# Turning tokens 1 and 3 of the last group in shifted blocks, with the other copy of the output weights, and a new issue order for the tail

## Chip, cores, metric

The kernel runs on one core of a Trainium2 chip. The metric is the device time of one launch in microseconds (us), the median of several runs; lower is better. About 0.2% (0.3 us) is what a measurement of this kernel can tell from no change.

## What is computed

Two independent layers over 2048 tokens of width 448 (bf16), their outputs side by side in one `[1, 2048, 896]` tensor. Part A is a diagonal state-space layer (448 complex states, a scan over the sequence, projections in and out, a skip term). Part B is local attention with 16 heads of width 28, where each token looks at 8 keys spaced 2 apart:

```
# part A
h   = Lam_bar * h + B_bar @ x[t]                 # for t in 0..2047, complex
y   = 2 * real(C @ h) + x * Dskip
# part B
q, k, v = split_heads(x @ wqkv)                  # 16 heads, 28 wide
idx     = pos[:, None] - 2 * arange(8)           # masked where negative
p       = softmax(q . k[idx] / sqrt(28))         # over the 8 keys
o       = sum_w p[w] * v[idx[w]]
b       = merge_heads(o) @ wo
out     = concat([y, b], -1)
```

## The kernel before, in words

**Tiling.** Partition p of an on-chip tile holds the tokens 16p to 16p+15, so the kernel speaks of 16 "tokens" j = 0..15, each a row of 448 numbers on 128 partitions. Part B works on four groups of four tokens: g = 3 (tokens 12 to 15), 2, 1 and 0, in that order.

**Part B's last stages** (`PartB.pv`, L787). For each group VectorE (DVE in the profile) forms attention times values and adds the products up: `mul` (L819) and `add` (L822) work on 3584 columns, two halves ("y") of 4 tokens x 448, and at the end the halves would be added (L838). For groups 3, 2 and 1 a DMA then transposes the sum (`trd`, L872, issued by SyncE, SP in the profile), and TensorE (PE) multiplies the result by the output weights (`rr` L900 and `mm` L908). For group 0, the last, there is no time for a DMA: its last addition is cut in two (L841, part 0 for tokens 0 and 1, part 1 for tokens 2 and 3), and TensorE turns each token itself (`tr`, L884): four blocks of 128 columns, each by two matmuls against the identity, which also add the two halves. ScalarE (ACT) copies the turned token from PSUM (`ev`, L889), TensorE multiplies it by the output weights (`mm`, L915, four matmuls), ScalarE copies the product out (`ev2`, L218 in the helper; for token 2 VectorE takes the last 192 columns, L222), and SyncE sends it away (`out`, L925).

448 columns are three blocks and a half. Before, token j's four blocks start at column 448j, so the fourth reaches 64 columns into the next token, and `wo_p[:, 3]` has zeros in its lower 64 rows, where those columns fall. `wo_p` holds a second copy of the weights in rows 4 to 7, displaced by 64, which groups 1 to 3 already use for odd tokens.

**Part A's end** (`PartA.outputs`, L1443). For each token, or pair of tokens, TensorE sums up `y_ps` (L1458, L1462), ScalarE copies it out (L218), or for tokens 12 to 15 VectorE adds the skip term while it copies (L1474, after L1439 has made the term from `Dskip`, loaded at L1429); SyncE sends it (L1477).

**PSUM.** One buffer of two banks (tag "W") and six of one bank (tag "s"). Every `y_ps`, `pt_o` (a turned token) and `wo_ps` (a product with the output weights) takes one of the six or the "W"; a matmul into a reused bank waits until the engine that emptied it is done.

**Order.** Each piece of work is a numbered unit, and `ORDER` (L51) lists all 685 by hand. The program is built in that order, so each engine executes its units in the order in which they stand there, and waits by semaphores for the others. Each engine is a queue: a unit that waits holds up all behind it.

Of the kernel before, what the change touches and what calls it, by code (L numbers as in the profile page):

```python
# [10 lines left out]
ALU = mybir.AluOpType  # L11
# [28 lines left out]
NC = 3  # L40
# [6 lines left out]
ADD = (0, 0, 0, 0, 0, 0, 0)  # L47
EADD = (0, 0, 0, 0)
# [51 lines left out]
def vec2(n):  # L100
    return n / 1920.0 + 0.07
# [219 lines left out]
class PartB:  # L321
# [464 lines left out]
    def pv(self, b, prio, deps):  # L786
# [13 lines left out]
        lasts, halves, trs = {}, {}, {}  # L800
        for r in (1, 0):
            last = getattr(self, "pv_last", None)
            half = getattr(self, "u_half", None)
            ahead = half is not None
            us = (5, 4, 1, 0)
            for n in range(4):

                def step(n=n, r=r, part=0, half=half):
                    alloc()
                    acc = self.acc[2 * b + r]  # L810
                    tmp = [acc] + [cx.pr[:, 4096 * i:4096 * i + 2 * n1] for i in range(3)]

                    def mul(i):
                        u = us[i]
                        o = j0 + 4 * r + DIL * u
                        w0 = 4 * (u // 4) + 2 * (u % 2)
                        aa = self.attn[b][:, w0:w0 + 2, :, r, :].rearrange("q y i h -> q (y i) h").unsqueeze(2).to_broadcast(
                            [NCH, 8, DH, H])
                        V.tensor_tensor(tmp[i].rearrange("p (j d h) -> p j d h", j=8, d=DH), aa, self.vd[:, o:o + 8], op=ALU.mult)  # L819

                    def add(i):
                        V.tensor_tensor(acc, acc, tmp[i], op=ALU.add)  # L822
                    if n == 0:
                        mul(1 if half else 0)
                        mul(2 if half else 1)
                    elif n == 1 and half:
                        mul(3)
                        mul(0)
                    elif n == 2 and half:
                        add(1)  # L830
                        add(2)
                    elif n < 3:
                        mul(n + 1)
                        add(n)
                    elif 2 * b + r > 0:
                        add(3)
                        if not EADD[2 * b + r]:
                            V.tensor_tensor(acc[:, n1:2 * n1], acc[:, 0:n1], acc[:, n1:2 * n1], op=ALU.add)  # L838
                    else:
                        a, t = (v.rearrange("p (y j c) -> p y j c", y=2, j=4)[:, :, 2 * part:2 * part + 2] for v in (acc, tmp[3]))  # L840
                        V.tensor_tensor(a, a, t, op=ALU.add)  # L841
                dd = []
                for u in us[:2 + ahead] if n == 0 else us[n + 1 + ahead:n + 2 + ahead] if n < 3 else ():
                    o = j0 + 4 * r + DIL * u
                    for p in range(o, o + 8):
                        dd += self.u_vh[p] if p < HALO else [self.u_v[p - HALO]]
                cost = 2 * vec2(2 * n1) if n < 3 else vec2(2 * n1) + vec2(n1) * (not EADD[2 * b + r]) if 2 * b + r > 0 else vec2(n1)
                last = P.add("DVE", cost, step, dd + [self.u_attn[b], last, *self.u_prod[0], *self.u_prod[1], *self.u_lg[0], *self.u_lg[1],
                                         *self.u_vm, *self.u_proj, *deps, half if n == 1 else None], prio - 0.1 * r)
            lasts[r] = [last, last]  # L850
            if 2 * b + r == 0:
                last = P.add("DVE", cost, lambda: step(part=1), [last], prio - 0.1 * r)
                lasts[r][1] = last
            self.pv_last = last
            g = 2 * b + r
            halves[g] = self.u_half = None
            if EADD[g]:

                def merge(g=g):
                    acc = self.acc[g]  # L860
                    nc.gpsimd.dma_start(acc[:, n1:2 * n1], acc[:, 0:n1], accum_op=ALU.add)
                halves[g] = self.u_half = P.add("POOL", 1.1, merge, [last], PRI["wo"], lat=3.5)
            if not hasattr(self, "u_first"):
                self.u_first = last
        for r in (1, 0):
            g = 2 * b + r
            if g > 0:

                def trd(g=g):
                    o = (0, 5376, 7168, 8960)[g]  # L870
                    t = self.oTd[g] = self.rb2[:, o:o + n1].rearrange("p (k q) -> p k q", q=NCH)
                    nc.sync.dma_start(t, self.acc[g][:, n1:2 * n1], transpose=True)  # L872
                trs[r] = P.add("SP", 1.7, trd, [halves[g] or lasts[r][1]], PRI["wo"], lat=3.6)
        for j in range(j0, j0 + JB):
# [3 lines left out]
            def tr(j=j, jb=jb):  # L878
                pt = jb["pt"] = self.psum.tile([NCH, KT, NCH], f32, name="pt_o", tag="s")
                a = j % 4 * D  # L880
# [22 lines left out]
            def mm(j=j, jb=jb, g=g, e=e):  # L903
# [10 lines left out]
                for kt in range(KT):  # L914
                    nc.tensor.matmul(ps[:], lhsT=o[:, kt, :], rhs=self.wo_p[:, kt, :],  # L915
                                     start=(kt == 0), stop=(kt == KT - 1))
# [27 lines left out]
class PartA:  # L944
# [261 lines left out]
    def scan(self, prio, qk_done):  # L1206
# [9 lines left out]
        for m in range(NM):  # L1216
# [99 lines left out]
            def carry(out, lt, Sc, hv, new=False):  # L1316
                mt(out[:, 0:NCH], lhsT=lt, rhs=Sc, start=new, stop=True, **kw)
                mt(out[:, NCH:512], lhsT=lt, rhs=hv[:, 3, 0:384], start=False, stop=True, **kw)
# [12 lines left out]
            def again(n, box=box, pair=pair):  # L1331
# [5 lines left out]

            def back(n, box=box, again=again, hget=hget):
                again(n)
                mt(box[2 * n], lhsT=cx.ident[:], rhs=hget()[:, 2 * n, :], start=True, stop=False, **kw)  # L1340

            def s6(box=box, Sc=Sc, L=L, hget=hget, again=again, add=bool(ADD[m])):
                if add:
                    again(0)
                carry(box[0], L(1), Sc, hget(), add)

            def s7(box=box, L=L, hget=hget, again=again, add=bool(ADD[m])):
                if add:
                    again(1)
                mt(box[2], lhsT=L(1), rhs=hget()[:, 1, :], start=add, stop=True, **kw)  # L1350

            def ctile(box=box):
                if "c" not in box:
                    box["c"] = pool.tile([NCH, 2, 512], bf16, name="cP", tag="cP", bufs=NC)
                return box["c"]

            def addin(box=box, hget=hget):
                nc.gpsimd.dma_start(hget()[:, 0::2, :], box["c"][:], accum_op=ALU.add)

            def evPf(box=box, hget=hget, ctile=ctile, add=bool(ADD[m])):  # L1360
                nc.scalar.copy(ctile()[:] if add else hget()[:, 0::2, :], box["P"][:])

            def evpf(n, box=box, hget=hget, ctile=ctile, add=bool(ADD[m])):
                nc.scalar.copy(ctile()[:, n, :] if add else hget()[:, 2 * n, :], box[2 * n])  # L1364
# [39 lines left out]
            add = bool(ADD[m])  # L1404
            if not hold[0] and not add:
                b0 = P.add("PE", pe(1, 512), lambda f=back: f(0), [b0], PRI["bk"] + m * 0.1, acq="W" if pair else "s")
            if not hold[pair ^ 1] and not add:
                b2 = P.add("PE", pe(1, 512), lambda f=back: f(1), [b2, b0], PRI["bk"] + m * 0.1, acq=None if pair else "s")
            v0 = P.add("PE", pe(2, 256), s6, [b0, u3], pc, acq=("W" if pair else "s", "cP") if add else None)
            v2 = P.add("PE", pe(1, 512), s7, [b2, u1, v0 if add and pair else None], pc, acq="s" if add and not pair else None)  # L1410
# [5 lines left out]
            if add:  # L1416
                w0 = w2 = P.add("POOL", 1.2, addin, [w0, w2], pc, rel="cP", lat=3.0)
# [91 lines left out]
def kernel(  # L1509
# [24 lines left out]
    plan = Planner({**BUFS, "fl": NF, "cP": NC, "PR": 3, "mx": 1, "ex": 1, "at": 1, "pw": 4, "oT": 3, "yb": 4, "ya": 8})  # L1534
# [64 lines left out]
```

## Time and profile before

| | |
|---|---|
| median of 3 runs | 139.94 us (139.92 to 139.99) |
| the profiled execution | 140.0 us, span of its instructions 138.3 us |
| busy: PE, DVE, ACT, POOL | 131.3, 123.0, 88.3, 17.7 us |
| mean granted TensorE clock | 0.997 |
| chain that ended last | DVE 39%, PE 38%, SP's queue 9%, issue 5% |
| last group's last addition (L841) ends | 128.57 us |
| last copy out of PSUM ends | 135.47 us |

The span goes from the first to the last instruction, so 1.7 us of the profiled execution lie around it. Positions below are microseconds from the span's start. In the chain of waits, "issue" is time in which the profile shows no cause; DVEq, SPq and so on are an engine's sequencer.

### The profile page before, as it was taken

To read this page: it belongs to the slowest core of one execution; us is meant where nothing else is said; L and a number is where in the kernel's file an instruction comes from. 1 tells how busy PE (TensorE), PEld (TensorE's weight loads), DVE (VectorE), ACT (ScalarE), POOL (GpSimd) and SP (SyncE) were. 2 spreads that over 40 slices of the span, in tenths; PEclk is the share of its full clock that TensorE was granted. 3 is DMA by queue.
4 is the path that set the end of the run, shared out by engine and by line. 5 is a ranking of instruction groups with operands and counts; after the bars stand their busy time and mean duration, and the time that the engine had idled before them with its cause. 6 is when DMAs were issued, how large, how long until landed. Compare 5 with 4: busy or idle time off the path is not lost.

```text
span 138.3 us, 2835 instructions
## 1 busy us (share of the span) xinstructions
PE 131.3 (95%) x1065; PEld 67.2 (49%) x1071; DVE 123.0 (89%) x134; ACT 88.3 (64%) x199; POOL 17.7 (13%) x69
## 2 busy tenths in 40 slices
PE   7999989999999999999999999999999999999790
PEld 2534334444455453656534563556565455445450
DVE  1369998899999999997999999999999999999920
ACT  3555587998554976657695998689547151721571
POOL 7589830025000000000000000000000000000000
PEclk9999999999999999999999999999999999999998
DMA  4968965658658525648899039350093425575163
GB/s 128 269 126 208 179 87 61 153 130 95 81 113 53 97 52 112 179 104 131 167 222 198 0 67 240 95 111 0 0 95 103 139 78 118 141 163 169 35 197 100
DMA packets 41694, 16.58 MB, mean 120 GB/s; under 512 B 33685, under 2 KB 41044, under 8 KB 41681
## 3 DMA queue, kind: packets, MB, share of 16 engines
q1 hardware_dynamic: 41618, 16.40, 57.6%
q8 instruction: 8, 0.13, 0.4%
q14 instruction: 5, 0.04, 0.1%
q10 hardware_dynamic: 63, 0.01, 0.0%
HBM read 4.32 MB, written 3.67 MB: 58 GB/s over the span
## 4 chain that ended last, share of the span: by engine, by line
DVE 39%; PE 38%; SPq 9%; issue 5%; ACT 3%; DMA 3%; DVEq 0%; ACTq 0%
DVE rb L822 11%; DVE prods L819 11%; SPq L366 6%; PE v_ps L760 6%; PE scb L1247 5%; DVE rb L819 4%; PE scp L1247 4%; PE logits L672 3%; DMA rb<-in_B_x_dram 3%; DVE pw L1197 2%; PE qk_ps L481 2%; DVE prods L656 2%; PE wo_ps L915 2%; DVE rb L838 2%; ACT qk L218 1%
## 5 line engine op out<-in xcount | busy, mean ns | idle before, releaser
L819 DVE TENSOR_TENSOR prods<-attn,vd 128x3584 bf16<-128x3584 bf16 x12 | 24.0, 2018 | 0.0
L822 DVE TENSOR_TENSOR rb<-rb,prods 128x3584 bf16<-128x3584 bf16 x11 | 22.2, 2019 | 0.1
L656 DVE TENSOR_TENSOR prods<-qk 128x3072 bf16<-128x3072 bf16 (+1 forms) x15 | 19.1, 1325 | 0.0
L481 PE MATMUL qk_ps<-rb 128*128 128x512 bf16 x60 | 14.4, 379 | 0.7 <-DMA rb<-in_B_x_dram 0.6
L1462 PE MATMUL y_ps<-Ccat,qk 128*128 128x448 bf16 x60 | 14.6, 352 | 0.0
L218 ACT CAST vd<-v_ps 128x448 bf16<-128x448 f32 x16 | 7.9, 540 | 5.2 <-PE v_ps L760 4.9
L1247 PEld LDWEIGHTS <-Bcat 128*128 128x128 bf16 x84 | 7.5, 100 | 7.4 <-issue 1.1
L1294 ACT CAST ubuf<-scb 128x64 bf16<-128x64 f32 x35 | 7.3, 220 | 5.9 <-PE scb L1301 3.5
L218 ACT CAST qk<-wo_ps 128x448 bf16<-128x448 f32 (+1 forms) x16 | 8.1, 529 | 4.5 <-PE wo_ps L908 2.8
L1462 PE MATMUL y_ps<-Ccat,h 128*128 128x448 bf16 x45 | 11.0, 353 | 0.0
L1247 PE MATMUL scb<-xaT_sb,Bcat 128*128 128x512 bf16 x42 | 10.9, 380 | 0.0
L218 ACT CAST qk<-y_ps 128x448 bf16<-128x448 f32 (+1 forms) x9 | 5.6, 663 | 8.2 <-issue 4.2
L760 PE MATMUL v_ps<-rb 128*128 128x448 bf16 x48 | 10.1, 353 | 0.0
L220 ACT ACTIVATE qk<-qk_ps 64x512 bf16<-64x512 f32 (+1 forms) x15 | 8.9, 599 | 1.7 <-PE qk_ps L488 1.3
L481 PEld LDWEIGHTS <-rb 128*128 128x128 bf16 x60 | 5.6, 98 | 7.8 <-issue 1.0
L660 DVE TENSOR_TENSOR prods<-qk 128x768 bf16<-128x768 bf16 (+3 forms) x18 | 9.1, 566 | 0.1
L1462 PEld LDWEIGHTS <-qk 128*128 128x128 bf16 x60 | 5.8, 98 | 5.3 <-ACT qk L1364 0.2
L819 DVE TENSOR_TENSOR rb<-attn,vd 128x3584 bf16<-128x3584 bf16 x4 | 8.1, 2021 | 0.1
L908 PE MATMUL wo_ps<-wo_p,rb 128*128 128x448 bf16 x36 | 8.1, 353 | 0.0
L1197 DVE TENSOR_TENSOR pw<-Dm,spair 128x1920 bf16<-128x1920 bf16 x7 | 8.1, 1150 | 0.0
L218 ACT CAST qk<-qk_ps 128x512 bf16<-128x512 f32 (+2 forms) x11 | 6.3, 585 | 2.5 <-PE qk_ps L488 1.1
L1247 PE MATMUL scp<-xaT_sb,Bcat 128*128 128x512 bf16 x30 | 7.8, 381 | 0.0
(197 smaller groups left out, 259.0 us busy)
## 6 DMA issues: line engine op xcount, KB each, us to landing
out_dram<-qk SPq DMA_DIRECT2D x32, 112.0 KB, 1.8
vd<-vd SPq DMA_DIRECT2D x3, 392.0 KB, 4.5
rb<-in_B_wqkv_dram SPq DMA_DIRECT2D x3, 336.0 KB, 4.5
qk<-in_A_x_dram SPq DMA_DIRECT2D x1, 448.0 KB
ra<-in_A_B_re_dram SPq DMA_DIRECT2D x1, 392.0 KB, 4.3
ra<-in_A_B_im_dram SPq DMA_DIRECT2D x1, 392.0 KB
rb<-in_A_C_re_dram SPq DMA_DIRECT2D x4, 98.0 KB, 2.9
rb<-in_A_C_im_dram SPq DMA_DIRECT2D x4, 98.0 KB, 3.5
```

What stands on the lines that cost most here:

```text
L218: nc.scalar.copy(out, in_)
L220: nc.scalar.mul(out, in_, scale)
L366: nc.sync.dma_start(self.xT[:, j], bass.AP(x.tensor, x.offset + j * D - DT, [[T * D, NCH], [1, KT * NCH]]), transpose=True)
L481: nc.tensor.matmul(out(n), lhsT=w(n, full, k), rhs=self.xT[:, j:j + 4, k, :], start=(not rfirst and k == 1), stop=(rfirst and k == KT - 1) ...
L656: V.tensor_tensor(out.rearrange("p i j k q -> p i (j k) q"), qq.unsqueeze(1).to_broadcast([NCH, 2, 4 * nk, NCH]), bass.AP(kk.tensor, kk.of ...
L660: V.tensor_tensor(jk(out[:, i, a:e]), qq, kk, op=ALU.mult)
L760: nc.tensor.matmul(box["ps"][:].rearrange("p h d -> p (h d)"), lhsT=self.xT[:, j, k, :], rhs=self.wv[:, k, :], start=False, stop=(k == KT ...
L819: V.tensor_tensor(tmp[i].rearrange("p (j d h) -> p j d h", j=8, d=DH), aa, self.vd[:, o:o + 8], op=ALU.mult)
L822: V.tensor_tensor(acc, acc, tmp[i], op=ALU.add)
L1197: V.tensor_tensor(t[:], self.o["Dm"][:].rearrange("p (a b) -> p a b", b=2).unsqueeze(1).to_broadcast([NCH, 2 * NPW, 32, 2]), self.sp[:, m ...
L1247: mt(box[i], lhsT=self.Bcat[:, k, m, :], rhs=self.xk(slice(i, None, 4), k), start=(i % 2 == 0 and k == 0), stop=False, **kw)
L1462: nc.tensor.matmul(ps, lhsT=h, rhs=self.Ccat[:, m, :], start=(m == 0 and not skip), stop=(m == NM - 1), skip_group_check=True)
```

## The change

Three things.

1. For tokens 1 and 3 of group 0 the four blocks start 64 columns earlier, at 448j - 64. The first block now begins in the token before, and the fourth ends with the token. The product uses rows 4 to 7 of `wo_p`. Token 1 then reads nothing of tokens 2 and 3. The number of instructions is the same.
2. The last nine lines of `ORDER` are rearranged. Group 0's tokens are turned in the order 0, 2, 1, 3 (1, 2, 3, 0 before), and outputs of part A, products of groups 1 to 3 and transfers change places.
3. Two options that the tables switch off for all steps (`ADD`, `EADD`, and the buffer `cP`) are taken out. They issued nothing.

```diff
-ADD = (0, 0, 0, 0, 0, 0, 0)
-EADD = (0, 0, 0, 0)
...
 ORDER = [
...
-    443, 405, 462, 463, 407, 440, 441, 409, 464, 465, 445, 402, 442, 466, 467, 444, 530, 403, 446, 404, 468,
+    443, 405, 462, 463, 407, 440, 441, 409, 464, 465, 445, 402, 442, 466, 467, 444, 530, 570, 531, 616, 403,
...
             def tr(j=j, jb=jb):
                 pt = jb["pt"] = self.psum.tile([NCH, KT, NCH], f32, name="pt_o", tag="s")
-                a = j % 4 * D
+                a = j % 4 * D - 64 * (j % 2)
...
                 for kt in range(KT):
-                    nc.tensor.matmul(ps[:], lhsT=o[:, kt, :], rhs=self.wo_p[:, kt, :],
+                    nc.tensor.matmul(ps[:], lhsT=o[:, kt, :], rhs=self.wo_p[:, 4 * (j % 2) + kt, :],
                                      start=(kt == 0), stop=(kt == KT - 1))
...
-                        if not EADD[2 * b + r]:
-                            V.tensor_tensor(acc[:, n1:2 * n1], acc[:, 0:n1], acc[:, n1:2 * n1], op=ALU.add)
+                        V.tensor_tensor(acc[:, n1:2 * n1], acc[:, 0:n1], acc[:, n1:2 * n1], op=ALU.add)
```

What the order of issue becomes, at three places. Line numbers of the changed kernel are 20 lower in the second half of `pv` (L884 becomes L864, L908 L888, L915 L895), 38 lower in `outputs`, 3 lower in the helper (L218 becomes L215).

First place, TensorE's last stretch, before. The numbers tell tiles apart: `pt_o_1792`, `1809`, `1825`, `1841` are tokens 1, 2, 3, 0 turned; `wo_ps_1744` is token 7's product, `wo_ps_1819`, `1853`, `1861`, `1868` are the products of tokens 1, 2, 3, 0. In brackets stand the engines whose semaphores the instruction waits for.

```order
L884 MATMUL pt_o_1792<-ident_63,rb_70 128x128 [waits Activation_49]
...
L884 LDWEIGHTS rb_70 [waits DVE_49]
...
L908 MATMUL wo_ps_1744<-wo_p_587,rb_70 128x448
...
L884 MATMUL pt_o_1809<-ident_63,rb_70 128x128 [waits Activation_49]
...
L915 MATMUL wo_ps_1819<-wo_p_587,rb_70 128x448 [waits DVE_49]
...
L884 MATMUL pt_o_1825<-ident_63,rb_70 128x128 [waits PE_49]
...
L884 MATMUL pt_o_1841<-ident_63,rb_70 128x128 [waits DVE_49]
...
L915 MATMUL wo_ps_1853<-wo_p_587,rb_70 128x448
...
L915 MATMUL wo_ps_1861<-wo_p_587,rb_70 128x448
...
L915 MATMUL wo_ps_1868<-wo_p_587,rb_70 128x448 [waits PE_49]
```

The same stretch now: `pt_o_1788`, `1806`, `1820`, `1830` are tokens 0, 2, 1, 3 turned; `wo_ps_1740` is token 7's product, `wo_ps_1815`, `1842`, `1852`, `1868` the products of tokens 0, 2, 1, 3.

```order
L864 MATMUL pt_o_1788<-ident_63,rb_70 128x128 [waits Activation_49]
...
L888 MATMUL wo_ps_1740<-wo_p_587,rb_70 128x448
...
L864 LDWEIGHTS rb_70 [waits DVE_49]
L864 MATMUL pt_o_1806<-ident_63,rb_70 128x128 [waits Activation_49]
...
L895 LDWEIGHTS rb_70 [waits Activation_49]
...
L864 MATMUL pt_o_1820<-ident_63,rb_70 128x128 [waits DVE_49]
...
L864 MATMUL pt_o_1830<-ident_63,rb_70 128x128 [waits PE_49]
...
L895 MATMUL wo_ps_1842<-wo_p_587,rb_70 128x448
...
L895 LDWEIGHTS rb_70 [waits DVE_49,Activation_49]
L895 MATMUL wo_ps_1852<-wo_p_587,rb_70 128x448
...
L895 MATMUL wo_ps_1868<-wo_p_587,rb_70 128x448 [waits PE_49]
```

Before, the first wait for VectorE that is not for the sum itself stands after two turned tokens, and one more turned token stands behind a second such wait. Now two turned tokens and a whole product stand ahead of the first, and the second stands ahead of the product of token 1.

Second place, ScalarE's last copies, before: `wo_ps_1626` is the product of token 11 (group 2).

```order
L218 CAST qk_109<-wo_ps_1740 128x448
L889 CAST rb_70<-pt_o_1792 128x512
L218 CAST qk_109<-wo_ps_1626 128x448
L218 CAST qk_109<-wo_ps_1744 128x448
L889 CAST rb_70<-pt_o_1809 128x512
L218 CAST qk_109<-wo_ps_1819 128x448
L889 CAST rb_70<-pt_o_1825 128x512
L889 CAST rb_70<-pt_o_1841 128x512
L218 CAST qk_109<-wo_ps_1853 128x256
L218 CAST qk_109<-wo_ps_1861 128x448
L218 CAST qk_109<-wo_ps_1868 128x448
```

And now:

```order
L215 CAST qk_109<-wo_ps_1739 128x448
L869 CAST rb_70<-pt_o_1788 128x512
L215 CAST qk_109<-wo_ps_1740 128x448
L869 CAST rb_70<-pt_o_1806 128x512
L215 CAST qk_109<-wo_ps_1815 128x448
L869 CAST rb_70<-pt_o_1820 128x512
L869 CAST rb_70<-pt_o_1830 128x512
L215 CAST qk_109<-wo_ps_1842 128x256
L215 CAST qk_109<-wo_ps_1852 128x448
L215 CAST qk_109<-wo_ps_1868 128x448
```

Token 11's copy is gone from this stretch: TensorE makes its product right behind those of tokens 12, 8 and 9, and ScalarE copies it there.

Third place, SyncE's queue where group 0's attention weights are transposed (L727, L724 now), before:

```order
L774 DMA vd_620<-vd_620 15x1792
L727 DMA_TRANSPOSE attn0_1484<-attn_t_1394 128x8x128
L925 DMA out_0_dram<-qk_109 128x448
L872 DMA_TRANSPOSE rb_70<-rb_70 128x14x128
...
L1477 DMA out_0_dram<-qk_109 128x448 x7
```

And now:

```order
L771 DMA vd_620<-vd_620 15x1792
L905 DMA out_0_dram<-qk_109 128x448
L1391 DMA rb_70<-in_A_Dskip_dram 128x448
L724 DMA_TRANSPOSE attn0_1500<-attn_t_1394 128x8x128
L852 DMA_TRANSPOSE rb_70<-rb_70 128x14x128
L1439 DMA out_0_dram<-qk_109 128x448 x6
```

The transpose of the attention weights now stands behind an output and the load of `Dskip`. Further on, ten outputs stand ahead of the transpose of group 1 (L872), where after that of group 2 nine stood before. VectorE's own order is the same.

More of the change, by code (lines that the diff above doesn't have):

```diff
@@ L39 @@
 NF = 3
-NC = 3
 WARM = 6
@@ L799, in pv, with step @@
         self.oTd = getattr(self, "oTd", {})
-        lasts, halves, trs = {}, {}, {}
+        lasts, trs = {}, {}
         for r in (1, 0):
             last = getattr(self, "pv_last", None)
-            half = getattr(self, "u_half", None)
-            ahead = half is not None
             us = (5, 4, 1, 0)
             for n in range(4):
-                def step(n=n, r=r, part=0, half=half):
+                def step(n=n, r=r, part=0):
                     alloc()
@@ L823, in step @@
                     if n == 0:
[L824 to L827, printed above, removed]
                         mul(0)
-                    elif n == 2 and half:
-                        add(1)
-                        add(2)
+                        mul(1)
                     elif n < 3:
@@ L842, in pv @@
                 dd = []
-                for u in us[:2 + ahead] if n == 0 else us[n + 1 + ahead:n + 2 + ahead] if n < 3 else ():
+                for u in us[:2] if n == 0 else us[n + 1:n + 2] if n < 3 else ():
                     o = j0 + 4 * r + DIL * u
@@ L846, in pv @@
                         dd += self.u_vh[p] if p < HALO else [self.u_v[p - HALO]]
-                cost = 2 * vec2(2 * n1) if n < 3 else vec2(2 * n1) + vec2(n1) * (not EADD[2 * b + r]) if 2 * b + r > 0 else vec2(n1)
+                cost = 2 * vec2(2 * n1) if n < 3 else vec2(2 * n1) + vec2(n1) if 2 * b + r > 0 else vec2(n1)
                 last = P.add("DVE", cost, step, dd + [self.u_attn[b], last, *self.u_prod[0], *self.u_prod[1], *self.u_lg[0], *self.u_lg[1],
-                                         *self.u_vm, *self.u_proj, *deps, half if n == 1 else None], prio - 0.1 * r)
+                                         *self.u_vm, *self.u_proj, *deps], prio - 0.1 * r)
             lasts[r] = [last, last]
@@ L854, in pv @@
             self.pv_last = last
[L855 to L862, printed above, removed]
             if not hasattr(self, "u_first"):
@@ L872, in trd @@
                     nc.sync.dma_start(t, self.acc[g][:, n1:2 * n1], transpose=True)
-                trs[r] = P.add("SP", 1.7, trd, [halves[g] or lasts[r][1]], PRI["wo"], lat=3.6)
+                trs[r] = P.add("SP", 1.7, trd, [lasts[r][1]], PRI["wo"], lat=3.6)
         for j in range(j0, j0 + JB):
@@ L1314, in ev3, with carry @@
                 nc.scalar.copy(hget()[:, 3, 0:384], box[3][:, 0:384])
-            def carry(out, lt, Sc, hv, new=False):
-                mt(out[:, 0:NCH], lhsT=lt, rhs=Sc, start=new, stop=True, **kw)
+            def carry(out, lt, Sc, hv):
+                mt(out[:, 0:NCH], lhsT=lt, rhs=Sc, start=False, stop=True, **kw)
                 mt(out[:, NCH:512], lhsT=lt, rhs=hv[:, 3, 0:384], start=False, stop=True, **kw)
@@ L1329, in ev1f, with back @@
                 nc.scalar.copy(hget()[:, 1, :], box[1])
-            def again(n, box=box, pair=pair):
+            def back(n, box=box, pair=pair, hget=hget):
                 if pair and n == 0:
@@ L1336, in again, with s6, s7, evPf @@
                     box[2 * n] = self.psum.tile([NCH, 512], f32, name="scp%d" % (2 * n), tag="s")[:]
-            def back(n, box=box, again=again, hget=hget):
-                again(n)
                 mt(box[2 * n], lhsT=cx.ident[:], rhs=hget()[:, 2 * n, :], start=True, stop=False, **kw)
[L1342 to L1364, printed above, removed]
+            def s6(box=box, Sc=Sc, L=L, hget=hget):
+                carry(box[0], L(1), Sc, hget())
+            def s7(box=box, L=L, hget=hget):
+                mt(box[2], lhsT=L(1), rhs=hget()[:, 1, :], start=False, stop=True, **kw)
+            def evPf(box=box, hget=hget):
+                nc.scalar.copy(hget()[:, 0::2, :], box["P"][:])
+            def evpf(n, box=box, hget=hget):
+                nc.scalar.copy(hget()[:, 2 * n, :], box[2 * n])
             dx = [self.u_bc[m], u_pw, u_pad]
@@ L1403, in scan @@
             b0 = b2 = eh
-            add = bool(ADD[m])
-            if not hold[0] and not add:
+            if not hold[0]:
                 b0 = P.add("PE", pe(1, 512), lambda f=back: f(0), [b0], PRI["bk"] + m * 0.1, acq="W" if pair else "s")
-            if not hold[pair ^ 1] and not add:
+            if not hold[pair ^ 1]:
                 b2 = P.add("PE", pe(1, 512), lambda f=back: f(1), [b2, b0], PRI["bk"] + m * 0.1, acq=None if pair else "s")
-            v0 = P.add("PE", pe(2, 256), s6, [b0, u3], pc, acq=("W" if pair else "s", "cP") if add else None)
-            v2 = P.add("PE", pe(1, 512), s7, [b2, u1, v0 if add and pair else None], pc, acq="s" if add and not pair else None)
+            v0 = P.add("PE", pe(2, 256), s6, [b0, u3], pc)
+            v2 = P.add("PE", pe(1, 512), s7, [b2, u1], pc)
             if pair:
@@ L1415, in scan @@
             done[m] = P.add("POOL", 0.0, lambda: None, [w0, w2, u1], rel=("fl", "pw"), lat=0.0)
-            if add:
-                w0 = w2 = P.add("POOL", 1.2, addin, [w0, w2], pc, rel="cP", lat=3.0)
             self.u_h.append((w0, u1, w2, [u3, eh]))
@@ L1533, in tile @@
             return psum.tile(shape, dtype, name=name, tag=tag, bufs=BUFS[tag])
-    plan = Planner({**BUFS, "fl": NF, "cP": NC, "PR": 3, "mx": 1, "ex": 1, "at": 1, "pw": 4, "oT": 3, "yb": 4, "ya": 8})
+    plan = Planner({**BUFS, "fl": NF, "PR": 3, "mx": 1, "ex": 1, "at": 1, "pw": 4, "oT": 3, "yb": 4, "ya": 8})
     ctx.enter_context(tc.manual_schedule())
```

16 rows, old and new, of the table ORDER are left out of this document.

## Prediction

> **What bounds the kernel now.** First the page's busy times: two engines are nearly full, so the question is which of them sets the end and when.
>
> ```profile
> span 138.3 us, 2835 instructions
> PE 131.3 (95%) x1065; PEld 67.2 (49%) x1071; DVE 123.0 (89%) x134; ACT 88.3 (64%) x199; POOL 17.7 (13%) x69
> ```
>
> Then the chain that ended last, in order of time, its last 9 us (start, length, what):
>
> ```profile
> 126.48 0.04 DVE rb L841
> 126.52 0.97 issue
> 127.49 1.10 DVE rb L841
> 128.59 0.04 issue
> 128.63 0.29 PE pt_o L884 x2
> 128.92 0.57 PE wo_ps L908 x3
> 129.49 0.45 PE pt_o L884 x8
> 129.94 0.09 issue
> ...
> 130.15 0.17 issue
> 130.32 1.62 DVE qk L1474 x2
> 131.94 0.04 issue
> 131.98 0.61 PE pt_o L884 x8
> 132.59 2.28 PE wo_ps L915 x12
> 134.88 0.03 ACTq L218
> 134.90 0.04 issue
> 134.94 0.53 ACT qk L218
> ```
>
> VectorE carries the path up to 128.59, where part 1 of the last sum ends. After that the path isn't TensorE's work alone: at 129.94 it goes back to VectorE, to the skip additions of tokens 12 to 15 (L1474), and only at 131.98 to the fourth turned token, token 0. The timeline of that stretch shows why (start, length, engine, line; in brackets the idle time before and what ended it):
>
> ```profile
> 127.63 0.51 PE L884 MATMUL pt_o<-ident,rb 128*128 128x128 bf16 x6
> 128.63 0.29 PE L884 MATMUL pt_o<-ident,rb 128*128 128x128 bf16 x2 [0.49 <-DVE rb L841]
> 128.76 0.73 PE L908 MATMUL wo_ps<-wo_p,rb 128*128 128x448 bf16 x3
> 128.96 0.59 ACT L889 CAST rb<-pt_o 128x512 bf16<-128x512 f32 x1 [3.89 <-PE pt_o L884]
> 129.32 0.61 PE L884 MATMUL pt_o<-ident,rb 128*128 128x128 bf16 x8
> 129.44 0.97 ACT L218 CAST qk<-wo_ps 128x448 bf16<-128x448 f32 x2
> 129.78 2.15 DVE L1474 TENSOR_TENSOR qk<-y_ps,qk 128x448 bf16<-128x448 f32 x3 [0.20 <-DVE qk L1439]
> 130.46 0.92 PE L915 MATMUL wo_ps<-wo_p,rb 128*128 128x448 bf16 x4 [0.52 <-ACT qk L218]
> 131.98 0.61 PE L884 MATMUL pt_o<-ident,rb 128*128 128x128 bf16 x8 [0.17 <-DVE qk L1474]
> 132.43 2.43 PE L915 MATMUL wo_ps<-wo_p,rb 128*128 128x448 bf16 x12
> 134.94 0.53 ACT L218 CAST qk<-wo_ps 128x448 bf16<-128x448 f32 x1 [0.23 <-PE wo_ps L915]
> ...
> L1474 DVE TENSOR_TENSOR qk<-y_ps,qk x3: 614/623/1080, 129.8 to 131.3; 128x448 bf16<-128x448 f32 x2, 128x896 bf16<-128x896 f32 x1
> ```
>
> TensorE stands still three times. At 128.63 token 1's fourth block waits for part 1 of the sum. At 130.46 the product of token 1 waits; the row names ScalarE, which finished at 130.41, but the order of issue says that this matmul waits for VectorE, and the first L1474 (0.62 us, token 15) ended at 130.40: a PSUM bank. At 131.98 token 0 waits for the bank of token 14, the third L1474, ended at 131.93. From there on nothing waits: 8 and 12 matmuls, a copy, a transfer. The end is thus set by the time at which VectorE empties token 14's bank, plus the work that stands behind it in TensorE's queue.
>
> **The change, part by part.**
>
> *The shift by 64 columns.* As many instructions of the same sizes, so no work is added or removed. What goes is the wait of 0.49 us at 128.63 for token 1. But both the old token 1 and the new one meet the bank of token 15 at 130.46 anyway, 0.5 us after TensorE had run dry in spite of that wait. Without the reordering I put its worth at zero: the stall would only move to 130.46. It is still what lets tokens 0 and 1 be turned without part 1 of the sum, in whichever order. Reading rows 4 to 7 of the weights instead of 0 to 3 I cost at nothing, since `mm` on odd tokens (L908) reads them already: 3 matmuls at 0.187 each, whatever the copy.
>
> *The options taken out.* Nothing was issued; zero.
>
> *The order of the last turned tokens.* This is the term. I follow TensorE's new queue with the distances of the rows above: a 128-column matmul every 0.056 (8 in 0.45, the chain's third PE row), a 448-column one every 0.187 (12 in 2.43 with the last one's 0.35 latency), a result 0.16 behind the next issue. Token 0 needs part 0 of the sum only, so its first block starts at 127.63 as token 1's did, and its last is issued at 128.08. Token 7's product takes 0.56, to 128.64. Token 2 needs part 1 (128.59) and is just in time: to 129.09. ScalarE has copied token 0 by 128.87 (128.28 and 0.59), so its product runs from 129.09 to 129.84. Now token 1 has to take token 15's bank: 130.46, as in the row above. Tokens 1 and 3: 0.90, to 131.36. Then three products, of tokens 2, 1 and 3, 12 matmuls in 2.24, to 133.60, the last result at 133.77 (132.43 + 2.43 = 134.86 before). Token 14's bank is now wanted by the product of token 1, at 132.11, and is free at 131.93, so it decides no more, by 0.18.
>
> In short: before, the last release was at 131.93, with one turned token and three products behind it. Now it is at 130.40, with two turned tokens and three products behind it. That is 1.53 earlier, and 0.45 more to do: 1.08, or 1.09 by the two ends (134.86 and 133.77). ScalarE's last copy follows 0.08 later and takes 0.53, so it ends at 134.38 instead of 135.47. Behind it nothing changes:
>
> ```profile
> 134.18 1.66 SPq L925 DMA_DIRECT2D out_dram<-qk x3
> SPq L1594 <- DMA out_dram<-qk: 1.4, 1, 1.4
> ```
>
> The third issue of that row ends at 135.84, SyncE then waits 1.4 for the landing, and the rest to 138.3 is the program's end; the three outputs come a product (0.75) apart before and now, so SyncE, with about 0.4 an issue, doesn't pace them.
>
> Why there is room for a product ahead of the first wait: of the six banks two are held by tokens 14 and 15 until VectorE is done. Before, a third was held by token 11's product, which ScalarE copied only in the tail; it is made and copied some 16 us earlier now. I cost that at nothing there: the same 3 matmuls and one copy of 0.53 move, and ScalarE idled 3.89 us ahead of its copy at 128.96, above.
>
> *The reordering farther up.* VectorE's order is unchanged, so part 1 ends at 128.6 unless VectorE starves; TensorE does the same matmuls before token 0 as before token 1, so it arrives as before unless it meets a new wait. Bounds: none of it can come earlier than VectorE allows, so no gain; TensorE may come 0.62 late (130.46 less 129.84) before anything is lost. The pauses at the wide products (L900) are the nearest rows for a new wait, 0.37 each:
>
> ```profile
> 120.76 0.11 PEld L900 LDWEIGHTS <-rb 64*128 64x128 bf16 x4 [0.37 <-DVE prods L819]
> 114.78 1.40 SPq L872 DMA_TRANSPOSE rb<-rb x1
> rb<-rb SPq DMA_TRANSPOSE x3, 4.2
> 112.00 0.97 ACT L218 CAST qk<-wo_ps 128x448 bf16<-128x448 f32 x2
> ```
>
> One more is covered, two cost 0.12, three 0.49. I take zero and put 0.5 into the range. VectorE's copy of tokens 12 and 13 now writes two rows apart instead of side by side; it moves as many numbers, and I take its 1.08 us; 0.18 of extra time would be covered by the slack of token 14's bank. On the other side, VectorE's 0.20 idle before 129.78 could go (`Dskip` comes earlier), which would give 0.2.
>
> A rule that speaks against more stalls in the tail: TensorE's last stretch has a row of its own.
>
> ```profile
> 126.50:138.30 11.80, 7.18 (x58) 4.03 (x55) 5.59 (x7) 4.99 (x10) 0.00 (x0) 0.97 0.34 108
> ```
>
> PE is busy 7.18 of 11.80 us there, with three stalls, and the granted clock is still 0.97; 12 matmuls behind the third stall take 2.43. The Trainium skill ("TensorE: Matmul & The Clock Gate", "A second HAM failure mode: psum-queue depth-cycling") says that small pauses between groups of matmuls as banks cycle can make the clock gate swing between half and full rate. This trace doesn't show it with stalls of about 0.5 us each, and the new order has one stall of about 0.62 instead of three; if the rule held here, the sum would be that of the last rival below.
>
> **The rivals.**
>
> *Part of it is lost (14%).* ScalarE is strictly in order, and its list in the tail is now token 0, product 7, token 2, product 0, token 1, token 3. If a late copy holds the product of token 1 beyond 132.11, or TensorE arrives more than 0.62 late, the end slips by as much. For it: PE is at 95%, its slack is small. Against: token 1's copy would be ready at 131.70 (131.07 + 0.04 + 0.59), 0.4 early. With 0.3 to 0.7 lost: 139.15 to 139.55.
>
> *No change (4%).* If VectorE's three copies came 1.1 later, say because one waits for its target rows, whose earlier outputs have to have landed, the gain would be gone: 139.9. Against: those outputs are issued several us ahead, and an output lands in about 1.8 (the row below), while VectorE comes at 129.78.
>
> ```profile
> out_dram<-qk SPq DMA_DIRECT2D x32, 112.0 KB, 1.8
> ```
>
> *Slower, by the transpose of group 1 (5%).* Ten outputs stand ahead of it in SyncE's queue. It was issued at 114.78, behind the sum, landed about 4.2 later, at 119.0, and was wanted at 120.76. If token 11's or token 9's copy came late, SyncE would hold it. Everything behind it in TensorE's queue would shift: the first 1.76 are free, then 0.62, then the gain of 1.09 is eaten; it turns to slower from 118.25 on, and 1 us more costs 1 us: 140.9 at 119.25. Against: the two copies of such products ended at 112.97, and there are now four, 0.45 apart, so the last comes at about 114, just when the sum is done.
>
> *Slower, by the clock gate (2%).* If the new stall set TensorE to half rate for the rest, 0.90 + 2.24 would double: 3.1 later, less 1.09, so about 142.
>
> **How the numbers follow.** The profiled execution took 140.0, 1.7 more than its span, and the median is 139.94, so I take 0.06 off. Likeliest (75%): 140.0 - 1.09 - 0.06 = 138.85. Its own bounds are 138.6 (the idle 0.20 gone) to 139.1. The range reaches down to 138.5 and up through the larger part of the first rival to 139.4; outside lie the losses beyond that, no change and slower, some 15%. What differs by under 0.2% (0.28 us), either side of 139.94, is no change to a measurement. Faster: 75% + 12% of the first rival's 14%, so 0.87. Same: 4% and the rest of the first rival, 0.06. Slower: 0.07.
>
> **What would show it.** In the changed kernel's timeline: token 0's eight turning matmuls together from 127.6 without a pause; a product of four (L895) before 130; the one stall of the tail ending at about 130.46, right behind VectorE's first skip addition; then 16 turning matmuls and 12 products in a row; ScalarE's last copy ending at about 134.4. VectorE's L841 (L829 now) must still end at 128.6. The forecast is wrong if that moves, if TensorE reaches token 0 later than 128.2, or if the chain of waits at the end still goes through VectorE's third skip addition.

## The result and the profile after

| | before | changed |
|---|---|---|
| median | 139.97 us (139.92 to 140.22, 4 runs) | 138.63 us (138.48 to 138.87, 4 runs) |
| ratio, 95% interval | | 0.9902 [0.9883, 0.9922] |
| profiled execution | 140.0 us | 138.48 us |
| last sum (L841, now L829) ends | 128.57 | 128.11 |
| last copy out of PSUM ends | 135.47 | 133.93 |
| from the one to the other, "the tail" below | 6.90 | 5.82 |

The changed kernel is 1.3 us faster, 138.63 where 138.85 was forecast. The page of the changed kernel begins:

```profile
span 136.8 us, 2838 instructions
PE 131.0 (96%) x1066; PEld 67.2 (49%) x1071; DVE 123.1 (90%) x134; ACT 88.3 (65%) x199; POOL 17.5 (13%) x69
```

The engines do the same work as before; the span is shorter by 1.5 us. The chain that ended last, its last 8 us:

```profile
127.03 1.08 DVE rb L829
128.11 1.01 DVE qk L1401
...
129.32 0.63 DVE qk L1436
129.95 0.04 issue
130.00 1.05 PE pt_o L864 x16
131.05 2.28 PE wo_ps L895 x12
...
133.40 0.53 ACT qk L215
```

It now leaves VectorE at the first skip addition (L1436, 0.63 us, token 15) instead of the third, and 16 turning and 12 product matmuls follow in a row. The timeline of the same stretch:

```profile
127.17 0.62 PE L864 MATMUL pt_o<-ident,rb 128*128 128x128 bf16 x8
127.63 0.73 PE L888 MATMUL wo_ps<-wo_p,rb 128*128 128x448 bf16 x3
128.19 0.61 PE L864 MATMUL pt_o<-ident,rb 128*128 128x128 bf16 x8
128.64 0.92 PE L895 MATMUL wo_ps<-wo_p,rb 128*128 128x448 bf16 x4
129.32 2.15 DVE L1436 TENSOR_TENSOR qk<-y_ps,qk 128x448 bf16<-128x448 f32 x3 [0.20 <-DVE qk L1401]
130.00 1.05 PE L864 MATMUL pt_o<-ident,rb 128*128 128x128 bf16 x16 [0.43 <-DVE qk L1436]
130.88 2.43 PE L895 MATMUL wo_ps<-wo_p,rb 128*128 128x448 bf16 x12
```

One stall is left in the tail, at 130.00. The tail is 1.08 us shorter. The other 0.46 us of this one profile (128.57 against 128.11) arose before VectorE's long run of products and sums began. The chain of waits at 14 to 25 us of three executions shows it, before, changed, and the changed kernel in a later run:

```profile
14.61 3.48 DMA rb<-in_B_x_dram
18.34 2.75 PE qk_ps L481 x12
24.57 0.04 DVE prods L654
```

```profile
14.59 3.04 DMA rb<-in_B_x_dram
17.88 2.75 PE qk_ps L478 x12
24.11 0.04 DVE prods L651
```

```profile
14.58 4.01 DMA rb<-in_B_x_dram
18.84 2.75 PE qk_ps L478 x12
25.07 0.04 DVE prods L651
```

A transposing load of part B's input landed 3.48, 3.04 and 4.01 us after its issue, TensorE's projection (`qk_ps`) waits for it, and VectorE's product of queries and keys (`prods`) starts at 24.57, 24.11 and 25.07. The change touches nothing there, and the last two views are of the same program. Not every execution hangs on this load: in four of the thirteen profiles of this study the chain to that product runs through TensorE's own matmuls almost from the start, in one of the four behind a load of weights, and the product starts at 24.51 to 24.72. From that product's start to the end of the last sum VectorE takes 104.01 to 104.03 us in every profile of this study, and from the last copy to the end of the execution 4.50 to 4.57 us pass. A profiled time is thus the start of the product, 104.0, the tail and 4.5, and the tail alone can be read without the scatter of the first 25 us.

### The profile page after: what moved, and what is told of

Same layout as the page of the kernel before. It is cut to its first block, busy times and chain, and to the rows that moved or that the text cites. A ratio compares the mean times of both kernels' runs of the same rounds, so it can differ in the third digit from the quotient of the medians.

```text
span 136.8 us, 2838 instructions
## 1 busy us (share of the span) xinstructions
PE 131.0 (96%) x1066; PEld 67.2 (49%) x1071; DVE 123.1 (90%) x134; ACT 88.3 (65%) x199; POOL 17.5 (13%) x69
## 4 chain that ended last, share of the span: by engine, by line
DVE 39%; PE 38%; SPq 10%; issue 5%; ACT 3%; DMA 2%; DVEq 0%; ACTq 0%
DVE rb L817 12%; DVE prods L814 11%; SPq L363 7%; PE v_ps L757 6%; PE scb L1227 5%; DVE rb L814 4%; PE scp L1227 4%; PE logits L669 3%; DVE pw L1177 2%; DMA rb<-in_B_x_dram 2%; PE qk_ps L478 2%; DVE prods L653 2%; PE wo_ps L895 2%; DVE rb L826 2%; ACT qk L215 1%
## 5 line engine op out<-in xcount | busy, mean ns | idle before, releaser
L215 ACT CAST qk<-wo_ps 128x448 bf16<-128x448 f32 (+1 forms) x16 | 8.2, 527 | 10.0 <-PE wo_ps L888 7.8
L215 ACT CAST vd<-v_ps 128x448 bf16<-128x448 f32 x16 | 7.9, 540 | 5.2 <-PE v_ps L757 4.9
L888 PE MATMUL wo_ps<-wo_p,rb 128*128 128x448 bf16 x36 | 8.1, 353 | 0.0
L215 ACT CAST qk<-qk_ps 128x512 bf16<-128x512 f32 (+2 forms) x11 | 6.3, 585 | 2.3 <-PE qk_ps L485 1.1
L215 ACT CAST qk<-y_ps 128x448 bf16<-128x448 f32 (+1 forms) x9 | 5.6, 662 | 3.1 <-PE y_ps L1424 3.1
```

Of the source, the lines that this page charges most:

```text
L215: nc.scalar.copy(out, in_)
```

## The experiments

Medians are compared with the kernel before on the same chip: 140.11 us for the first four rows below it, 140.04 for the next four, 140.24 for the last three. "Start" is the start of that product on VectorE in the profiled execution; it belongs to that one execution and not to the median.

| kernel | median | ratio to before | start | tail |
|---|---|---|---|---|
| before | | | 24.57 | 6.90 |
| shift alone | 140.05 | 0.9998 [0.9986, 1.0009] | 24.39 | 6.90 |
| order alone | 138.96 | 0.9916 [0.9902, 0.9929] | 24.51 | 5.82 |
| changed | 139.18 | 0.9933 [0.992, 0.9946] | 25.07 | 5.82 |
| token 11 early alone | 139.13 | 0.9932 [0.9917, 0.9946] | 24.72 | 5.89 |
| changed, once more | 139.04 | 0.9924 [0.991, 0.9937] | 24.67 | 5.82 |
| token 11 early and shift | 138.77 | 0.9909 [0.9896, 0.9923] | 24.71 | 5.82 |
| before, banks emptied by ScalarE | 139.04 | 0.9922 [0.9908, 0.9937] | 24.74 | 5.89 |
| changed, banks emptied by ScalarE | 138.52 | 0.9892 [0.9879, 0.9906] | 24.63 | 5.22 |
| the same once more | 138.48 | 0.9866 [0.9842, 0.989] | 25.06 | 5.22 |
| the same without the shift | 138.68 | 0.9877 [0.9856, 0.9899] | 24.52 | 5.22 |
| before, banks emptied by ScalarE, shift | 138.43 | 0.9869 [0.9846, 0.9893] | 24.54 | 5.22 |

**The changed kernel again**, as a measure for the others.

> The changed kernel once more, beside the others of this study. Theory (a PSUM bank): 1.09 us of its gain come from the tail, measured from the end of the last sum to the last copy out of PSUM (6.90 us before, 5.82 in its first profile), and come again; the other 0.25 of its first median (138.63 against the 138.85 forecast) come from the loads in the first 25 us, which the change doesn't touch, and may or may not come again: 138.5 to 138.9. Rival: the reordering farther up is worth 0.25 by itself; then the last sum ends earlier relative to the first product of VectorE.

The gain is 0.93 us; in a second group of runs, with the expectation below, 1.00. The 139.18 misses the 138.5 to 138.9 that was expected, while the tail came again as expected. With the first comparison's 1.34 these are three measurements (ratios 0.9902, 0.9933 and 0.9924) of a tail that is 1.08 shorter in each of the three profiles. The stretch from the product to the last sum is as long as before in each, so the rival, a gain from the reordering farther up, shows nothing; what differs between the profiles lies in the first 25 us. Ratios 0.3% apart can thus be of the same program, so 0.2% is less than one such comparison can tell.

> The changed kernel as it is, as the measure for the three others. Theory (the last bank that VectorE empties before TensorE's last work sets the end): 0.9 to 1.3 us below the kernel before; from the end of the last sum to the last copy out of PSUM 5.82 us, as in its first profile, against 6.90 before. Rival (the gain is only in the first 25 us, where loads come when they come): the stretch behind the last sum would differ from profile to profile by tenths.

**The shift alone.**

```
-                a = j % 4 * D
+                a = j % 4 * D - 64 * (j % 2)
...
-                    nc.tensor.matmul(ps[:], lhsT=o[:, kt, :], rhs=self.wo_p[:, kt, :],
+                    nc.tensor.matmul(ps[:], lhsT=o[:, kt, :], rhs=self.wo_p[:, 4 * (j % 2) + kt, :],
```

> The kernel before with only the shift by 64 columns and the other copy of the weights; its order of issue is the old one. Theory (a PSUM bank): the wait of 0.49 us for the second part of the sum goes, but the product of token 1 still waits for the bank that VectorE empties 1.8 us after that sum: 139.9, no change. Rival (the shift is the point): the 0.49 us are gained, 139.45. Second rival for the early 0.46: if the loads are faster in this one too, its first product of VectorE starts near 24.1 instead of 24.6 and it comes out at 139.5 to 139.7 with the tail unchanged at 6.9.

The tail is 6.90 as before. The timeline shows where the removed pause went (on this run's clock, 0.16 ahead of before at the last sum):

```profile
127.47 0.62 PE L884 MATMUL pt_o<-ident,rb 128*128 128x128 bf16 x8
...
128.49 0.61 PE L884 MATMUL pt_o<-ident,rb 128*128 128x128 bf16 x8
129.62 2.15 DVE L1474 TENSOR_TENSOR qk<-y_ps,qk 128x448 bf16<-128x448 f32 x3 [0.20 <-ACT qk L218]
130.39 0.92 PE L915 MATMUL wo_ps<-wo_p,rb 128*128 128x448 bf16 x4 [1.28 <-DVE qk L1474]
...
132.26 2.43 PE L915 MATMUL wo_ps<-wo_p,rb 128*128 128x448 bf16 x12
```

Token 1 is turned without a pause, and the wait for token 15's bank at 130.39 has grown to 1.28 us. The row of before put 0.52 there and named ScalarE; here VectorE is named.

**The order alone**, which is the changed kernel with the two lines above put back.

> The changed kernel without the shift: blocks of tokens 1 and 3 start at 448j again and use the first copy of the weights; the order of issue is the new one. Theory: tokens 1 and 3 are turned behind the bank's release, when both parts of the sum are long done, so nothing is lost: as the changed kernel, 138.6 to 138.9, tail 5.8. Rival (the shift is the point): 0.49 is lost, 139.1 to 139.4.

The tail is 5.82, as with the shift: the order brings all of the change's gain. Its median of 138.96 is just above the range expected. That it is 0.2 us below the changed kernel's doesn't show a cost of the shift, since the two tails are equal and the intervals of the two ratios overlap.

**Token 11 early alone.** Three numbers of the order of before, 554, 555 and 556, move up: token 11's product, copy and output; the rest of the list and the turning order 1, 2, 3, 0 stay:

```
-    649, 650, 654, 544, 545, 547, 548, 655, 558, 656, 484, 662, 665, 619, 573, 574, 575, 531, 549, 580, 663,
-    664, 666, 667, 668, 670, 552, 559, 671, 553, 561, 562, 620, 560, 661, 621, 622, 672, 576, 577, 674, 563,
-    578, 546, 579, 673, 602, 609, 682, 603, 604, 616, 623, 605, 610, 618, 611, 612, 669, 606, 679, 607, 608,
-    675, 554, 586, 587, 555, 556, 613, 614, 615, 591, 592, 588, 589, 597, 683, 684, 590, 598, 676, 680, 677,
+    649, 650, 654, 544, 545, 547, 554, 548, 555, 655, 558, 656, 484, 662, 665, 619, 573, 574, 575, 531, 549,
+    580, 556, 663, 664, 666, 667, 668, 670, 552, 559, 671, 553, 561, 562, 620, 560, 661, 621, 622, 672, 576,
+    577, 674, 563, 578, 546, 579, 673, 602, 609, 682, 603, 604, 616, 623, 605, 610, 618, 611, 612, 669, 606,
+    679, 607, 608, 675, 586, 587, 613, 614, 615, 591, 592, 588, 589, 597, 683, 684, 590, 598, 676, 680, 677,
```

> The kernel before with three units moved and nothing else: the product of token 11 with the output weights, its copy out of PSUM and its transfer stand behind those of tokens 8 and 9, as in the changed kernel, instead of in the tail. No shift, old order of turning (1, 2, 3, 0). Theory (one bank more in the tail): the product of token 1 no longer waits for token 15's bank, only the 0.49 us for the second part of the sum stay: TensorE's last matmul ends near 133.8 instead of 134.9, 138.9 to 139.0, a tail near 5.9. Rival (the order of turning tokens 0, 2, 1, 3 brings the gain): 139.9, no change.

The tail is 5.89, 1.01 of the 1.08. After the pause for part 1 of the sum (here at 128.79) nothing stands still:

```profile
128.79 0.29 PE L884 MATMUL pt_o<-ident,rb 128*128 128x128 bf16 x2 [0.49 <-DVE rb L841]
...
129.93 0.92 PE L915 MATMUL wo_ps<-wo_p,rb 128*128 128x448 bf16 x4
129.93 2.16 DVE L1474 TENSOR_TENSOR qk<-y_ps,qk 128x448 bf16<-128x448 f32 x3 [0.20 <-DVE qk L1439]
130.68 1.06 PE L884 MATMUL pt_o<-ident,rb 128*128 128x128 bf16 x16
```

Token 15's bank is free at 130.56, and TensorE comes for it at 130.68. One bank released earlier, by one copy of 0.53 us that ScalarE made in the tail before, is worth nearly all that the nine rearranged lines are. The median, 139.13, is 0.13 above the time expected.

Three units moved, so what else could it be? Not TensorE's time: token 11's product stood ahead of the wait for part 0 of the sum, and that wait is 0.40 us before and 0.41 here. And not ScalarE's time: with the shift alone ScalarE was done with the copies of tokens 11 and 7 at 129.58 (its row is 128.61 and 0.97), and TensorE still stood until 130.39; and below, with tokens 14 and 15 emptied by ScalarE, token 11's copy stays in the tail of the kernel before and the tail is 5.89 as well.

**Token 11 early and the shift**, both edits above.

> The kernel before with token 11's product, copy and output early (alone: 5.88 us from the last sum to the last copy, gain 0.98 us) and the shift by 64 columns. Theory: the shift takes away the stall of 0.49 us at part 1 of the sum, which now stood alone; but TensorE then comes to token 15's bank at 130.19 on the clock of the run without shift, where it is free at 130.56, so 0.4 of the 0.49 come back as a wait: 5.80 us, 0.05 to 0.1 us faster than without shift, as fast as the changed kernel. Rival (the shift is worth its whole stall once the banks are free): 5.4 us, 0.5 us faster.

The tail is 5.82 and the theory's wait is there, 130.56 being the end of the first skip addition:

```profile
130.61 1.05 PE L884 MATMUL pt_o<-ident,rb 128*128 128x128 bf16 x16 [0.43 <-DVE qk L1474]
```

So 0.07 us of the shift shows and the rest comes back as a wait for VectorE. With the same tail as the changed kernel, this is the same result by three moved units and the shift, with the tokens still turned in the order 1, 2, 3, 0.

**Banks emptied by ScalarE.** If VectorE's late emptying sets the end, another engine should lift the limit. Tokens 14 and 15 are copied out by ScalarE as soon as their products are done, and VectorE adds the skip term to the copy:

```
                 if js[0] < 2 * self.n0:
                     cx.copy(eng, o, ps)
+                elif len(js) == 1:
+                    cx.copy("ACT", o, ps)
...
+            def add(j=js[0]):
+                o = cx.ya_v[:, cx.ya_row[j]]
+                nc.vector.tensor_tensor(o, o, self.xd[:, j - 2 * self.n0], op=ALU.add)
```

with two new units for ScalarE in the order (in the changed order `604, 685, 682` and `611, 686, 612`). First in the changed kernel, and with it again as the measure of the third group:

> The changed kernel, but ScalarE copies the products of tokens 14 and 15 out of PSUM (two copies of 0.53 more, where it idles 2.2 us), and VectorE adds the skip term to the copies. Theory: the banks are free before TensorE asks for them, so the one stall left (129.40 to 130.00, 0.60) goes, and 16 turning and 12 product matmuls follow without a pause: 5.22 us from the last sum to the last copy, 0.6 us less than the changed kernel, ratio to it 0.9957. Rival (TensorE waits there for ScalarE's copies, or SyncE's outputs set the end): no gain, or up to 0.5 us lost, as the two copies of 0.53 push the ones behind them.

> The changed kernel with the two copies by ScalarE once more, as the measure for the two others: 5.23 us from the last sum to the last copy as before, 1.5 us below the kernel before, ratio 0.989.

The tail is 5.22, shorter by the 0.60 that was expected. ScalarE's last copy of a `y_ps` ends at 127.01 (126.45 and 0.56), and the 16 turning matmuls start at 129.93 without a pause. The chain that ended last no longer goes through VectorE in the tail:

```profile
127.73 0.58 PE pt_o L864 x8
128.32 0.57 PE wo_ps L888 x3
128.89 0.45 PE pt_o L864 x8
129.33 0.76 PE wo_ps L895 x4
130.09 0.89 PE pt_o L864 x16
130.98 2.28 PE wo_ps L895 x12
```

The time went from 139.04 for the changed kernel to 138.52 on the same chip, and the intervals of the two ratios don't overlap. This version beats both kernels; the two groups of runs put it 1.52 and 1.76 us below the kernel before, for a tail that is 1.68 shorter.

Then in the kernel before, with the order otherwise as it was and no shift:

> The kernel before, in its old order and without the shift, with the same two copies by ScalarE. Theory (it is the banks, not the order): the waits at 130.46 (0.52) and 131.98 (0.55 between the issue of one token and the next) go, the one of 0.49 for part 1 of the sum stays; TensorE then has 26 turning matmuls at 0.056 and 19 product matmuls at 0.187 from 128.63 on, 5.0 us, and the last copy ends some 0.9 us earlier than before: 5.9 to 6.0 us behind the last sum, gain 0.8 to 1.0 us without any reordering. Rival (the order of the turned tokens matters for itself): no gain.

Without any unit reordered the gain is 1.00 us, and only the pause for part 1 is left, by which the tail is 5.89 and not 5.22:

```profile
127.81 0.51 PE L884 MATMUL pt_o<-ident,rb 128*128 128x128 bf16 x6
128.81 0.29 PE L884 MATMUL pt_o<-ident,rb 128*128 128x128 bf16 x2 [0.49 <-DVE rb L841]
...
129.94 0.92 PE L915 MATMUL wo_ps<-wo_p,rb 128*128 128x448 bf16 x4
...
130.70 1.06 PE L884 MATMUL pt_o<-ident,rb 128*128 128x128 bf16 x16
```

The expectation had the sum of the two waits nearly right but not their sizes. From the time when the next matmul could have been issued, the rows of before give 129.77 to 130.46 (token 2's turning starts at 129.32, eight times 0.056) and 131.66 to 131.98 (token 3's starts at 131.21): 0.69 and 0.32, and 1.01 is what came out of the tail.

**The shift where no bank is late.** The last two kernels put the shift into this one, and take it out of the one before.

> The kernel before in its old order, with the two copies by ScalarE (alone: 5.89 us from the last sum to the last copy out of PSUM) and the shift by 64 columns. Theory: with the banks free the shift is worth its whole pause. In the run without it six turning matmuls start at 127.81 and are issued by 128.15, the other two start at 128.81: 0.66 lost. With the shift TensorE runs on: 5.89 - 0.66 = 5.23 us, as in the changed order with the two copies, and 0.6 us less than the same kernel without shift, near 138.5. Rival 1 (the shift is worth nothing, as it was alone and with token 11 early): 5.89 us, 139.0. Rival 2 (ScalarE, with eight copies in a row there, sets the pace in the old order): between, 5.4 to 5.8 us.

> The changed order with the two copies by ScalarE, without the shift. Theory: in this order tokens 0 and 2 are turned first, and token 0 needs part 0 of the sum alone, token 2 part 1, with or without shift; tokens 1 and 3 come after part 1 has ended. So the shift is worth nothing here: 5.23 us from the last sum to the last copy, the same time as with shift within 0.2 us. Rival (the other copy of the weights or the place of the columns counts): over 0.3 us apart.

In the old order the shift now takes the tail from 5.89 to 5.22, its whole pause:

```profile
127.61 0.62 PE L884 MATMUL pt_o<-ident,rb 128*128 128x128 bf16 x8
...
128.63 0.61 PE L884 MATMUL pt_o<-ident,rb 128*128 128x128 bf16 x8
```

In the new order it is worth nothing: the tail is 5.22 with and without, medians 138.48 and 138.68 with intervals that overlap. ScalarE's longer run of copies in the old order is no limit. The two orders give the same tail, 5.22, once the banks are free in time and no token waits for part 1.

## Why the prediction was right

**What sets the end.** The prediction said that VectorE's emptying of the banks of tokens 15 and 14, and the work behind that in TensorE's queue, set the end. That is shown: with the emptying moved to ScalarE the stalls go in both orders (tails 5.22 and 5.89). Those kernels differ otherwise only in where VectorE reads for the skip addition, and that addition is off the path there.

**The order, -1.09.** The tail measured -1.08. The prediction took the order of the turned tokens and token 11's early bank as one term. The runs split it: the bank alone gives 1.01 with the old order of turning, and the bank with the shift all of it. So the new order of turning is not needed for the gain; the room that the bank makes, which the prediction named, is. The changed kernel's times plus the 0.46 by which its profile is early also agree with the steps: the one stall ends at 130.46 as forecast, the twelve products start at 131.34 (131.36), and the last copy ends at 134.39 (134.38). Token 14's bank is free at 131.47 on the profile's own clock (129.32 and 2.15), the second product wants it after the first four of the twelve matmuls, at 130.88 + 0.75 = 131.63, and nothing waits there. The slack is 0.16 (0.18).

**The shift, zero by itself.** Right, and for the reason given: alone it turns a pause into a longer wait for token 15's bank (0.52 to 1.28), and it shows only where the banks are free and the order turns token 1 before part 1 of the sum is there. Token 0 does not need it, against what the prediction says: its fourth block reaches into token 1, which part 0 of the sum covers, and in the new order the tails are the same without the shift (5.82 and 5.22). The step that was mis-sized is the pause itself. The prediction took the 0.49 of the idle column. That column counts from the modelled end of the last matmul; from the time when the next one could have been issued (127.63 and six times 0.056) to 128.63 it is 0.66, and 0.67 is what came out of the tail in the old order. The sum held no part of it.

**What was put at zero.** Freeing token 11's bank early cost nothing: VectorE's stretch to the last sum is 104.01 in the profile before and in the one after, and TensorE waited for part 0 of the sum 0.40 us in both, so it isn't late. VectorE's 0.20 idle ahead of the skip additions did not go, and its wide copy still takes 1.08:

```profile
L1436 DVE TENSOR_TENSOR qk<-y_ps,qk x3: 614/624/1080, 129.3 to 130.9; 128x448 bf16<-128x448 f32 x2, 128x896 bf16<-128x896 f32 x1
```

**The rivals.** No late copy held the product of token 1: the twelve products ran in a row. For the transpose of group 1 the rows of the changed kernel are:

```profile
114.31 1.53 SPq L852 DMA_TRANSPOSE rb<-rb x1
120.68 0.11 PEld L880 LDWEIGHTS <-rb 64*128 64x128 bf16 x4 [0.37 <-issue]
```

It was issued 0.47 earlier than before on a clock that is 0.46 earlier, so the ten outputs did not hold it, and the pause of 0.37 did not grow. As for the clock, the stretch of the changed kernel has this row (the mean granted clock is the last figure but two):

```profile
126.50:136.80 10.30, 6.38 (x55) 3.63 (x53) 5.12 (x7) 4.66 (x9) 0.00 (x0) 1.00 0.38 123
```

It is 1.00 with the stall. The 0.97 of before was no mark of its stalls: the row there reaches on to the end of the span, and from 128.00 to 135.50, where all three stalls lie, the clock is 1.00 as well. In the shift-alone kernel, with 1.28 us of idling, it is 1.00 from 128.00 to 135.40, and twelve products take 2.43 us, as everywhere. The Trainium skill's rule of pauses between bank cycles ("TensorE: Matmul & The Clock Gate", "A second HAM failure mode: psum-queue depth-cycling") doesn't show at this size of pause.

**The median.** The 138.63 is 0.22 under the forecast, and the two later measurements, 139.18 and 139.04, are above it. The prediction's term was right to 0.01 in the tail; that the first median came out lower than forecast and the later ones higher is scatter, which the prediction didn't price. The three profiles of the changed kernel put it at the start: VectorE's product begins at 24.11, 24.67 and 25.07.

## What to carry to other kernels

When a matmul that reuses a PSUM bank waits, look at what stands ahead of the emptying copy in the queue of the engine that makes it. A bank that is emptied earlier, by moving a copy up (1.01 us here) or by giving it to an idle engine and doing the arithmetic later on the copy (1.01 in the old order, 0.60 more in the new one), can be worth as much as a new order of everything. A pause taken out ahead of such a wait was worth 0 to 0.07 us here, and 0.67 once the wait was gone, so try each edit with and without the other. And where a random part of the time lies in one stretch, measure the stretch that the change touches, from one fixed event to another: here tails agreed to 0.01 us where medians of the same program differed by 0.5.

## What the runs showed beside that

The transposing load on the chain took 3.04 and 4.01 us from its issue to landing in two executions of the same program, and VectorE's product started 0.96 us apart in them. In a third the chain there went through TensorE instead. This is the largest scatter seen in these profiles, and nothing here tried to take it away.

The skip addition is faster on the copy than out of PSUM: 0.39 against 0.62 us for 448 columns. The row is of the changed kernel with the banks emptied by ScalarE:

```profile
L1443 DVE TENSOR_TENSOR qk<-qk x2: 381/387/393, 129.7 to 131.0; 128x448 bf16<-128x448 bf16 x2
```

That agrees with the Trainium skill ("VectorE: DVE Perf Modes", "Why PSUM operands drop a tier"), by which an f32 operand in PSUM holds VectorE at its basic rate; the memory and the type changed together here, so the runs don't tell which of the two counts. It had no part in the gain, as the additions are off the path then.
